# Windowed attention and a squared-ReLU layer on one core: queries and keys of a pair get PSUM tiles of their own, and the first block gets another order

## The chip, the cores and the metric

The kernel runs on one core of one Trainium2 chip. Its time is the device time of one execution in microseconds (us), taken as the median of several runs. A profile of one execution stands beside it; its span runs from the first to the last instruction and is a little shorter than the time of the same execution. In the profile's rows PE is the matrix engine (TensorE), PEld its weight loads, DVE is VectorE, ACT is ScalarE, POOL is GpSimd, SP the engine that issues the DMAs here; SPq is SP's queue.

## The reference

```python
# q, k, v: (8, 8, 576, 64) float32;  w_in: (512, 2048), w_out: (2048, 512) float32
scores = q @ k.transpose(0, 1, 3, 2) / sqrt(64)
rel = pos[:, None] - pos[None, :]
scores = where((rel >= 0) & (rel < 64), scores, -1e9)      # causal, window of 64
attn = softmax(scores)                                     # over the last axis
x = (attn @ v).transpose(0, 2, 1, 3).reshape(4608, 512)    # heads side by side
h = maximum(x @ w_in, 0)
out = (h * h) @ w_out                                      # (4608, 512) float32
```

## The kernel before

**Tiles and blocks.** The 4608 tokens are cut into 36 tiles of 128 tokens. Two tiles make a pair (p = 0 to 17), two pairs a block of 512 tokens (g = 0 to 8). Pairs 8 and 15 are "tails": they hold the last 64 tokens of eight sequences and are loaded with more, smaller DMAs. Everything is computed in fp16 with sums in float32.

**Attention of a tile i.** Keys and queries are loaded, cast to fp16, and turned, so that the head dimension lies on the partitions. `S_` makes the scores: 16 small matmuls of 64x64, with keys as weights and queries as the moving operand. `expo` takes the exponential on ACT, `keep` lays the mask on it on DVE. (For tiles 0 to 3 the mask is instead added by two matmuls ahead of the scores.) `V` multiplies with the values, whose extra column of ones gives the sum; `norm` divides on DVE and writes x. Then x is turned, which gives xT, the moving operand of the first layer.

**How things are turned.** For pairs 0 to 6 (`AHEAD = 7`), `T` turns keys and queries on PE: 16 transposes into one PSUM tile of two banks, 8 for the keys, 8 for the queries. Four copies take them out, one for each tile's keys (`ck`, into kT) and queries (`cq`, into qT). The two tokens that lie side by side in a partition after the load must be put in order again. The key copy does that as it writes (neighbours in PSUM go to every second column). The query copy writes its columns as they come, and the tile is noted in `mixed`; `S_` then reads the queries of such a tile in steps of 64 elements. From pair 7 on, `dma_k` and `dma_q` turn keys and queries by DMA, and `S_` reads the queries in a row. In the same way x is turned on PE (`X`, then `copy_xT`) for tiles 0 to 15, that is for blocks 0 to 3, and by one DMA for each pair (`dma_xT`) from block 4 on.

**Two stages.** The first stage is a list of words, `FIRST`, written out by hand: each word is one step, with an optional engine behind a slash. The order of the words is the order of the instructions in each engine's queue; all DMAs are in SP's. The stage loads and scales `w_in` (`fw`, `w`), runs the attention of blocks 0 to 2, the first layer of blocks 0 and 1 (`U`, with `r` for the ReLU and `s` for the square), and the second layer of block 0 (`O`). `W` is a run of matmuls whose results nobody reads. The second stage is a loop over g = 2 to 9. In each round it lists events with a time between 0 and 1, sorts them and emits them: the second layer of block g-1 (`out_seven`, in 14 steps with its stores), the first layer of block g (16 calls of `UP`, from 0.05 on), the attention of block g+1, and the loads of pairs 2g+4 and 2g+5.

**What takes turns.** Scores, attention sums, turned keys and queries and turned x all draw on one PSUM pool of two tiles of two banks each (`ps_att`). The results of `U`, `O` and `W` draw in turn on two pools of two banks each (`either_pool`). Copies of one PSUM tile by ACT and DVE follow one another in program order.

**SP's order in a round g = 2** (x of block 3 is still turned on PE): turn pair 7 (0.06), load keys, queries and values of pair 8 (0.14), turn pair 8 (0.52), load pair 9 (0.60), store a half of block 1's output (about 0.82), store the other half (about 0.96). In the rounds from 3 on, the DMA that turns x stands at 0.275 and 0.735, behind the loads at 0.14 and 0.60.

The events of attention and of loading, as they stand in the loop:

```python
ev += [(t + 0.02, lambda a=a: sc(a)), (t + 0.021, lambda b=b: sc(b)),
       (t + 0.25, lambda a=a: va(a)), (t + 0.251, lambda b=b: va(b)),
       (t + dx, lambda a=a: to_xT(a)), (t + dx + 0.0001, lambda b=b: to_xT(b))]
...
ev.append((t + 0.06, lambda a=a: (dma_k(a), dma_q(a))))
...
ev.append((t + 0.14, lambda a=a: load(a + 1)))
```

Of the kernel before, what the change touches and what calls it, by code (L numbers as in the profile page):

```python
# [14 lines left out]

SQ_ACT = (0, 2, 4, 6, 8, 10, 12, 14)
FIRST = '''
fv2 fk0 fq0 vc2/D fq1 kc0/A fk1 kc1/A qc1/D fv1 qc0/D h0 T0 W7 qc2 fv0 vd2 fv3 cq0/A ck0/D fw2 ck1
qc3/D fw1 S0 vc1 cq1 kc3/A kc2 S1 W5 ea0 vc0/D fw3 vd0/D eb0 fw0 ea1 vd1/D V0 W5 eb1 n0 V1 T1 n1
h2 vc3/D X0 W9 cq3/A ck2/D ck3 cq2 x0 X1 h4 w2.0/P w2.2 S2 x1/A fq2 vd3 w2.1 S3 ea2 w2.3 eb2 U0.4  # L20
ea3 w1.2/P w1.1 w1.0/A w1.3 V2 U0.5 eb3 n2 V3 r0.5 U0.3 n3 r0.4 w3.2/P s0.4/A w3.0/P X3 X2 w3.3/A
x3 U0.2 x2 r0.3 fk2 s0.5 s0.3/A U1.4 w3.1 r0.2/D U1.6 r1.4 s0.2 U0.6 w0.3/P r1.6 w0.1 fq3 w0.0/A
U1.2 s1.4 s1.6/A r0.6/D qc5 fv4 U0.7 qc4/A s0.6 U1.7 r1.2/D kc5 kc4/A fv5 s1.2 r0.7 w0.2/P T2
r1.7/D fv7 qc6 U1.1 ck4 cq4 ck5/D vc4 S4 r1.1 s0.7 U1.3 fk3 vd4 e4 cq5 h6 U1.0 fk5 s1.7/A vc5 m4
r1.3 S5 vd5 s1.1 e5 V4 fq4 U0.1 h8 n4 qc7 r1.0 U1.5 s1.3/A m5 kc7 fv6 vc7/A r0.1/D V5 kc6 X4 n5
U0.0 fv8 x4/A s1.0/A X5 r0.0/D T3 fk4 x5/A r1.5/D s0.1/A U2.5 fq5 ck7 vc6 s1.5 cq7/A U2.2 qc9
ck6/D r2.5 vd7 s0.0 U2.0 s2.5/A vd6 cq6 fv9 r2.2 S7 r2.0/D S6 fo1 U2.4 e6 s2.2 fo0 s2.0 U2.7 e7
fo2 m6 fo3 U2.3 qc11 r2.4 m7 qc8 r2.7 V6 V7 s2.4/A n6 vc8 U2.1 s2.7/A kc9 n7 kc8/A X6 U2.6 r2.1 x6
r2.3/D kc10/A X7 T4 qc10/A x7 s2.1 s2.3/A o6 U3.0 r2.6/D ck9 fv10 kc11 U3.6 ck8 s2.6 o4 cq8/A
r3.0/D o7 U3.7 vc9/A cq9 s3.0/A vd9 h10 U3.2 r3.6/D r3.7/D U3.1 r3.2 o0 s3.7 s3.6/A T5 o5 r3.1 o2  # L30
U3.4 o1/A ck11/D o3 s3.2/A ck10/D U3.5 o11 fq6 s3.1/A cq10 vd8 U3.3 r3.4/D cq11 s3.4/A S8 o10
r3.5/D S10 e8 fv14 O2.0 s3.5 o12 h12 e10 O2.1 m8 vc10 fv12 O1.0 o8/A o13 m10 fv11 r3.3 vd10 V8
s3.3/A S9 n8 O0.0 o9/A ws0.1 e9 fv13 O1.1 o15/A fk6 O0.1 m9 o14/A O1.2 qc13/A fv15 vc11 vc14/A
vd11 S11 V10 e11 O0.2 n10 vc12/A O1.3 ws0.3 fkq15 ws0.2 kc12 ws1.1 X8 oe1 st1 X10 O2.2 m11 vc13/A
ws1.3 qc12/A O3.0 x8 vd13 ws2.1 kc13/A O3.1 fkq14 vc15 x10 V11 ws1.2 vd14 V9 n11 O0.3 n9 vd15 T6
qc15 ws0.0 O2.3 kc15 cq13/A ck12/D oe0 st0 vd12 O3.2 cq12 ck13 ws2.3 X9 kc14 X11 ws1.0 x9/A O3.3
qc14 oe2 st2 x11 ws2.0 oe3 st3 ws2.2
'''


# [1 line left out]
def kernel(  # L42
# [70 lines left out]
    def tail_seq(i):  # L113

        return 4 * TAILS.index(i // 2) + i % 2 * 2
# [25 lines left out]
    def two_tiles():  # L141
        return stage.tile([P, 2, H, D], FP32, name="kq_st", tag="st2", bufs=6)
# [18 lines left out]
        for n in range(2):  # L161
            sts[nm, 2 * p + n] = st[:, n]

    def fetch_tail(p):

        for nm, src in (("k", k), ("q", q), ("v", v)):
            for i in (2 * p, 2 * p + 1):
                b = tail_seq(i)
                if nm == "q":
                    if i % 2 == 0:  # L170
                        st = two_tiles()
                    sts[nm, i] = st[:, i % 2]
                    for n in range(2):
                        fetch_rows(sts[nm, i], src, b + n, S - 64, 64, 64 * n)
                else:
                    st = two_tiles()
                    sts[nm, i] = st
                    for n in range(2):
                        fetch_rows(st[:, n], src, b + n, S - 128)

# [172 lines left out]
    def att_bank(name, dtype=FP32):  # L355
        return ps_att.tile([P, 2, 512], FP32, name=name, tag="ps_a")

    scs, avs, xps, tps, mixed = {}, {}, {}, {}, set()

    def T(p):  # L360
        ps = att_bank("qkT_ps")[:].rearrange("p s f -> p (s f)").bitcast(FP16).rearrange(
            "p (s two a t) -> p s a two t", s=2, two=2, a=HP)
        for s, src in enumerate((k16s, q16s)):
            for n in range(2):
                for hp in range(HP):
                    nc.tensor.transpose(out=ps[:, s, hp, n, :],  # L366
                                        in_=src[p][:, n, 2 * hp:2 * hp + 2, :],
                                        identity=ident[:])
        tps[p] = ps

    def k_cols(i):
        c0 = 64 + i % 2 * P
        return kT_of(i // 2)[:, :, c0:c0 + P]

    def qT_of(p):
        if p not in qTs:
            qTs[p] = attw.tile([P, 2, HP, P], FP16, name="qT", tag="qT", bufs=3)
        return qTs[p]

    def q_cols(i):  # L380
        return qT_of(i // 2)[:, i % 2]

    def half_of(i, s):
        c0 = i % 2 * 64
        return tps[i // 2][:, s, :, :, c0:c0 + 64]

    def copy_kT(i, eng=nc.scalar):

        copy(eng, k_cols(i).rearrange("p a (t two) -> p a two t", two=2), half_of(i, 0))

    def copy_qT(i, eng=nc.vector):

        copy(eng, q_cols(i).rearrange("p a (two t) -> p a two t", two=2), half_of(i, 1))
        mixed.add(i)

    def flip(out, in_):
        nc.sync.dma_start_transpose(out=out, in_=in_)
# [15 lines left out]
    def S_(i):  # L413
        sc = att_bank("sc")
        scv = sc[:].rearrange("p a (h b t) -> p a h b t", h=HP, b=2)
        for a in range(2 if i < 4 else 0):
            nc.tensor.matmul(sc[:, a, :], ident[:], minus[i > 0], start=True, stop=False,
                             skip_group_check=True)
        for hp in range(HP):
            for blk in range(2):  # L420
                for hh in range(2):
                    r0 = 64 * hh
                    qT = q_cols(i)[r0:r0 + 64, hp, :]
                    if i in mixed:
                        qT = qT.rearrange("d (two b t) -> d b t two", two=2, b=2)[:, blk]
                    else:
                        qT = qT[:, 64 * blk:64 * blk + 64]
                    nc.tensor.matmul(scv[:, hh, hp, blk, :], keys(i, hp, r0, blk), qT,  # L428
                                     start=i >= 4, stop=True, skip_group_check=i < 4)
        scs[i] = sc  # L430
        pms[i] = attw.tile([P, 2, HP * 2 * 64], FP16, name="pm", tag="pm")
# [57 lines left out]
            h2s[g] = h2pool.tile([P, FFC, 512], FP16, name="h2", tag="h2")  # L489
        return h2s[g]  # L490

    hps_of, hr_of, turns = {}, {}, []

    def either_pool():
        turns.append(len(turns) % 2)
        return ((ps_up, "ps_u"), (ps_out, "ps_o"))[turns[-1]]


    def U(p, j):
# [92 lines left out]
    def out_seven(g):  # L592
# [112 lines left out]
        "fkq": fetch_kq,  # L705
        "fw": fetch_w_in, "fo": fetch_w_out, "w": scale_w_in,  "o": cast_w_out,
        "kc": cast_k, "qc": cast_q, "vc": cast_v, "vd": shift_v,
        "T": T, "ck": copy_kT, "cq": copy_qT, "h": halo,
        "S": S_, "e": expo, "ea": lambda i: expo(i, lo), "eb": lambda i: expo(i, hi),
        "m": keep, "ma": lambda i: keep(i, lo), "mb": lambda i: keep(i, hi),  # L710
        "V": V, "n": norm, "X": X, "x": copy_xT, 
# [11 lines left out]
    def attention(g):  # L723
        c = 4 * g
        ev = []
        dx = 0.34 if g == 3 else 0.275

        def sc(i):
            S_(i)
            expo(i)  # L730
            later(2, lambda: keep(i))
            tick()

        def to_xT(i):
            if g == 3:
                X(i)
                copy_xT(i)
                tick()
            else:
                if i % 2:  # L740
                    dma_xT(i // 2)

        def va(i):
            V(i)
            norm(i)
            tick()

        for h in range(2):
            a, b, t = c + 2 * h, c + 2 * h + 1, 0.46 * h + (0.1 if g == 3 else 0.0)
            ev += [(t + 0.02, lambda a=a: sc(a)), (t + 0.021, lambda b=b: sc(b)),  # L750
                   (t + 0.25, lambda a=a: va(a)), (t + 0.251, lambda b=b: va(b)),
                   (t + dx, lambda a=a: to_xT(a)), (t + dx + 0.0001, lambda b=b: to_xT(b))]
        return ev

    def load(p):
        if p in TAILS:
            fetch_tail(p)
        else:
            for nm in "kqv":
                fetch_two(nm, p)  # L760
        for i in (2 * p, 2 * p + 1):
            if p in TAILS:
                k16s["tail", i] = st16.tile([P, 2, H, D], FP16, name="k16", tag="k16")
                nc.gpsimd.tensor_copy(out=k16s["tail", i][:], in_=sts["k", i][:])
            else:
                cast_k(i)
        for i in (2 * p, 2 * p + 1):
            cast_q(i)
        for i in (2 * p, 2 * p + 1):
            if p in TAILS:  # L770
                for n, vv in enumerate((v_ods, v_evs)):
                    nc.gpsimd.tensor_copy(out=vv[i % NV][:, :, 0:D], in_=sts["v", i][:, n])
            else:
                cast_v(i)
                shift_v(i)

    def loads(p):

        ev = []
        for h in range(2):  # L780
# [3 lines left out]
                if a not in TAILS:  # L784
                    ev.append((t + 0.3, lambda a=a: halo_apart(a)))
            if a + 1 < NCK // 2:
                ev.append((t + 0.14, lambda a=a: load(a + 1)))
        return ev

    def even(steps):  # L790
# [46 lines left out]
```

## Time and profile before

| what | us |
|---|---|
| median of 4 runs (300.78 to 303.2) | 302.16 |
| time of the profiled execution | 303.2 |
| its span | 301.5 |
| PE busy | 284.8 |
| DVE busy | 211.8 |
| ACT busy | 186.9 |
| POOL busy | 115.2 |

The granted clock of PE was 0.999 over the span. The DMA engines were at 0.9 or more of their time up to about 60 us, at 0.6 from 60 to 80 us, and at 0.76 to 1.07 from 80 to 240 us.

Reading help: a row of the chain gives start, duration, and the instruction or DMA that the end of the run goes back to at that moment. A row of a timeline gives start, duration from the first to the last of a group, engine, line, operation and tiles. A busy PE row can hold matmuls that run slower than they might; so the rate of matmuls (duration by count) is looked at beside the busy time.

### The profile page before, as it was taken

The numbers are of one execution on the slowest core, as the hardware profiler recorded it, in microseconds if no ns is written. First come the engines' busy times: TensorE is split into PE (matmuls) and PEld (weight loads), VectorE is DVE, ScalarE is ACT, GpSimd is POOL, SyncE is SP. The second block draws the span as 40 slices with busy tenths as digits, with TensorE's granted clock in tenths as the row PEclk, the third lists the DMA queues.
The fourth block names the chain that finished last, engine by engine and source line by source line (L and its number), as shares of the span: only waits on it lengthen the run. The fifth ranks groups of instructions, "written<-read, shape, count | busy, mean of one in ns | idle before, by whom it ended". The sixth has DMA issues, their size and how long they took to land.

```text
span 301.5 us, 7455 instructions
## 1 busy us (share of the span) xinstructions
PE 284.8 (94%) x3026; PEld 196.7 (65%) x3026; DVE 211.8 (70%) x407; ACT 186.9 (62%) x303; POOL 115.2 (38%) x172
## 2 busy tenths in 40 slices
PE   1989999999999999999999999959999999999995
PEld 0658888855566676666666666636666666666684
DVE  4678888866879568685877578765685867646393
ACT  3557798795484757757675767545757675566510
POOL 1359854683615172745266225350565000000000
PEclk9999999999999999999999999999999999999999
DMA  7999999993399999996998899999999211300133
GB/s 222 324 393 301 284 276 364 309 251 80 123 211 217 166 252 197 205 235 186 229 197 196 158 205 163 217 195 225 223 224 257 64 37 35 140 1 0 72 105 107
DMA packets 151843, 57.64 MB, mean 191 GB/s; under 512 B 128256, under 2 KB 143616, under 8 KB 151808
## 3 DMA queue, kind: packets, MB, share of 16 engines
q1 hardware_dynamic: 151808, 57.16, 78.4%
q8 instruction: 24, 0.39, 0.6%
q14 instruction: 11, 0.09, 0.1%
HBM read 38.80 MB, written 9.44 MB: 160 GB/s over the span
## 4 chain that ended last, share of the span: by engine, by line
PE 90%; DMA 3%; ACT 3%; DVE 2%; issue 0%; SPq 0%; DVEq 0%
PE hps L533 32%; PE opsC L621 9%; PE hps L505 9%; PE opsA L621 9%; PE opsD L621 8%; PE opsB L621 5%; PE sc L428 4%; PE ops L581 4%; PE av L451 4%; PE qkT_ps L366 2%; DMA q_st<-in_q_dram 2%; DMA xT<-x_sb 1%; PE xt_ps L471 1%; ACT kT L270 1%; DVE kT L272 1%; ACT pm L434 1%
## 5 line engine op out<-in xcount | busy, mean ns | idle before, releaser
L533 PE MATMUL hps<-xT,w_in_sb 128*128 128x512 f16 x448 | 112.9, 379 | 4.0 <-DMA xT<-x_sb 3.6
L537 ACT ACTIVATE hrelu<-hps 128x512 f32<-128x512 f32 x112 | 66.8, 597 | 71.8 <-PE hps L533 71.8
L621 PEld LDWEIGHTS <-h 128*128 128x128 f16 x624 | 60.5, 98 | 20.9
L533 PEld LDWEIGHTS <-w_in_sb 128*128 128x128 f16 x448 | 42.3, 98 | 36.8 <-issue 4.4
L543 DVE SCALAR_TENSOR_TENSOR h<-hps,hrelu 128x512 f16<-128x512 f32 x56 | 38.6, 690 | 33.7 <-ACT hrelu L537 33.4
L272 POOL COPY v_od<-v_ev 64x512 f16<-64x512 f16 x52 | 35.0, 675 | 12.2 <-ACT v_ev L270 9.3
L434 ACT ACTIVATE pm<-sc 128x1024 f16<-128x1024 f32 (+1 forms) x40 | 35.6, 936 | 3.9 <-PE sc L428 3.7
L540 ACT ACTIVATE h<-hrelu 128x512 f16<-128x512 f32 x56 | 35.2, 629 | 1.5
L621 PE MATMUL opsA<-w_out_sb,h 128*128 128x256 f16 x240 | 31.0, 273 | 0.0
L621 PE MATMUL opsD<-wb_all,h 128*128 128x256 f16 x240 | 30.9, 273 | 0.0
L621 PEld LDWEIGHTS <-hs_all 128*128 128x128 f16 x256 | 25.0, 98 | 8.6
L505 PE MATMUL hps<-xT,w_in_sb 128*128 128x256 f16 x256 | 30.5, 273 | 0.0
L272 POOL CAST k<-kq_st 128x512 f16<-128x512 f32 x18 | 11.3, 628 | 46.3 <-DMA kq_st<-in_k_dram 46.2
L505 PEld LDWEIGHTS <-w_in_sb 128*128 128x128 f16 x256 | 24.1, 98 | 3.3 <-DVE w_in_sb L274 0.2
L460 DVE TENSOR_TENSOR x_sb<-av,rden 128x512 f16<-128x512 f32 x36 | 24.9, 692 | 1.2
L439 DVE TENSOR_TENSOR pm<-pm,mask_inner 128x1024 f16<-128x1024 f16 x25 | 18.0, 721 | 4.9 <-ACT pm L434 4.9
L272 POOL CAST q<-kq_st 128x512 f16<-128x512 f32 x22 | 14.0, 638 | 12.4 <-DMA kq_st<-in_q_dram 11.7
L643 DVE SCALAR_TENSOR_TENSOR osb_all<-opsD,u 128x512 f32<-128x512 f32 x14 | 9.7, 691 | 11.3 <-PE opsD L621 11.3
L621 PE MATMUL opsC<-w_out_sb,h 128*128 128x256 f16 x128 | 16.4, 273 | 0.0
L621 PE MATMUL opsC<-w_out_sb,hs_all 128*128 128x256 f16 x128 | 16.4, 273 | 0.0
L621 PE MATMUL opsB<-wb_all,hs_all 128*128 128x256 f16 x128 | 16.4, 273 | 0.0
L459 DVE RECIPROCAL rden<-av 128x8 f32<-128x8 f32 x36 | 7.3, 202 | 12.5 <-PE av L451 12.3
(101 smaller groups left out, 377.6 us busy)
## 6 DMA issues: line engine op xcount, KB each, us to landing
kq_st<-in_k_dram SPq DMA_DIRECT2D x26, 256.0 KB, 3.6
kq_st<-in_v_dram SPq DMA_DIRECT2D x24, 256.0 KB, 4.7
out_dram<-osb_all SPq DMA_DIRECT2D x12, 512.0 KB, 3.2
kq_st<-in_q_dram SPq DMA_DIRECT2D x18, 256.0 KB, 4.3
v_st<-in_v_dram SPq DMA_DIRECT2D x16, 256.0 KB, 4.8
k_st<-in_k_dram SPq DMA_DIRECT2D x7, 512.0 KB, 5.5
q_st<-in_q_dram SPq DMA_DIRECT2D x7, 512.0 KB, 6.4
out_dram<-osb_all SPq DMA_DIRECT2D x11, 256.0 KB, 2.4
```

Source lines behind the costliest of these rows:

```text
L272: eng.tensor_copy(out=out, in_=in_)
L428: nc.tensor.matmul(scv[:, hh, hp, blk, :], keys(i, hp, r0, blk), qT, start=i >= 4, stop=True, skip_group_check=i < 4)
L434: nc.scalar.activation(out=pms[i][:, part], in_=scs[i][:, part], func=AF.Exp, scale=1.0 / float(D) ** 0.5)
L439: nc.vector.tensor_tensor(out=pms[i][:, part], in0=pms[i][:, part], in1=mask[:].rearrange("p (o a) r -> p o (a r)", o=1) .to_broadcast([P, ...
L451: nc.tensor.matmul(avs[i][64 * blk:64 * blk + 64, h // 4, h % 4, 0:65], pms[i][:, h % 2, h0:h0 + 64], vv[:, h, 0:65], start=True, stop=True)
L460: nc.vector.tensor_tensor(out=xs[i // 2][:, i % 2], in0=avs[i][:, :, :, 0:D], in1=rden[:].to_broadcast([P, 2, 4, D]), op=ALU.mult)
L505: nc.tensor.matmul(hps[:, f, :], w_in_sb[:, c, (2 * j + f) * P:(2 * j + f + 1) * P], xT_of(p // 2)[:, n0:n0 + 2, c, :], start=(c == 0), st ...
L533: nc.tensor.matmul(hps[:], w_in_sb[:, c, f * P:(f + 1) * P], xT_of(g)[:, :, c, :], start=(c == 0), stop=(c == DMC - 1))
L537: nc.scalar.activation(out=hrelu[:], in_=hps[:], func=AF.Relu)
L540: later(2 if f == 0 else 0, lambda: nc.scalar.activation(out=h2_of(g)[:, f, :], in_=hrelu[:], func=AF.Square))
L543: nc.vector.scalar_tensor_tensor(out=h2_of(g)[:, f, :], in0=hps[:], scalar=0.0, in1=hrelu[:], op0=ALU.max, op1=ALU.mult)
L621: nc.tensor.matmul(rows_of(bank, m), a[:, kk, m * P:(m + 1) * P], w[:, kk], start=(first and kk == 0 and (m == 0 or bank in apart)), stop= ...
```

## The change

- `T` is split into `Tk` and `Tq`. Keys keep a tile of the attention pool, of which they use one bank; queries get a bank of the two pools of `U`, `O` and `W`. Both halves are taken out by one copy of 1024 columns for a pair, where there were two of 512.
- The query copy now puts the columns in order as the key copy does, and `S_` reads the queries of every tile in a row; `mixed` is gone.
- `FIRST` is another order, with other engines for some words. `Tk1` stands right behind `Tk0`, the loads of both pairs' keys come before those of the queries, and there are 42 `W` matmuls in place of 26. In both orders the first `U` follows the scores of tiles 2 and 3. `fkq14` and `fkq15` (the loads for pair 7) stand behind the stores of two tiles.
- In the loop, x of block 3 is turned by DMA (`g == 99` is never true): 16 transposes on PE and 4 copies on DVE go, two DMAs come, at 0.375 and 0.835 of round 2.
- `load` is cut in two. Keys and queries are loaded at 0.14 and 0.60, for a tail pair the keys alone; the rest at 0.30 and 0.76. In rounds from 3 on, that is behind the DMA that turns x (0.275, 0.735); in round 2 the rest stands ahead of it.

The core of the diff, with the start of the new order:

```diff
+fv3 fk0 fk1 W9 vc3 fq0 kc0/D kc1/A fq1 h0 vd3/D Tk0 W3 kc3/A kc2 fv1 ck0 Tk1 W8 qc0 qc1/D fv0 h2
+ck1 Tq0 W11 fv2 cq0 qc2/A fw3 qc3/D S0 fw2 vc1/D fw1 S1 W5 ea0 fw0 vc0/D eb0 vd0/D ea1 vc2 vd1/D
+V0 eb1 Tq1 vd2 n0 cq1/A V1 W3 n1 X0 W3 x0 X1 S3 x1/A w3.0 w3.3/A fq2 w3.1 S2 w3.2 ea3 eb3 U0.6 ea2
+V3 eb2 U0.7 n3 w2.1/A w2.3/A w2.0 V2 w2.2 r0.6 X3 n2 U0.5 r0.7 s0.6/A s0.7 X2 U0.4 x2/A x3 w1.0/P
...
+    def T(p, nm):
+        if nm == "k":
+            bank = att_bank("kT_ps")[:, 0, :]
+        else:
+            pool, tag = either_pool()
+            bank = pool.tile([P, 512], FP32, name="qT_ps", tag=tag)[:]
+        ps = bank.bitcast(FP16).rearrange("p (a two t) -> p a two t", a=HP, two=2)
+        for n in range(2):
+            for hp in range(HP):
+                nc.tensor.transpose(out=ps[:, hp, n, :],
+                                    in_={"k": k16s, "q": q16s}[nm][p][:, n, 2 * hp:2 * hp + 2, :],
+                                    identity=ident[:])
+        tps[p, nm] = ps
...
+    def copy_kT(p, eng=nc.scalar):
+        copy(eng, kT_of(p)[:, :, 64:].rearrange("p a (t two) -> p a two t", two=2), tps[p, "k"])
+    def copy_qT(p, eng=nc.vector):
+        copy(eng, qT_of(p)[:].rearrange("p a (t two) -> p a two t", two=2), tps[p, "q"])
...
-                    if i in mixed:
-                        qT = qT.rearrange("d (two b t) -> d b t two", two=2, b=2)[:, blk]
-                    else:
-                        qT = qT[:, 64 * blk:64 * blk + 64]
+                    qT = qT[:, 64 * blk:64 * blk + 64]
...
-        dx = 0.34 if g == 3 else 0.275
+        dx = 0.34 if g == 99 else 0.275
...
-            if g == 3:
+            if g == 99:
                 X(i)
                 copy_xT(i)
...
-                ev.append((t + 0.14, lambda a=a: load(a + 1)))
+                kq = "k" if a + 1 in TAILS else "kq"
+                ev.append((t + 0.14, lambda a=a, x=kq: load(a + 1, x)))
+                ev.append((t + 0.3, lambda a=a, x=kq: load(a + 1, "kqv"[len(x):])))
```

## The prediction, made before the result was known

> **What bounds the kernel now.** First the busy table of the page, then PE's waits, then the chain, then SP's queue.
>
> ```profile
> PE 284.8 (94%) x3026; PEld 196.7 (65%) x3026; DVE 211.8 (70%) x407; ACT 186.9 (62%) x303; POOL 115.2 (38%) x172
> ```
>
> ```profile
> PE qkT_ps L366 <- ACT k L270: 6.2, 1, 6.2
> PE hps L533 <- DMA xT<-x_sb: 3.6, 1, 3.6
> PE xt_ps L471 <- DVE qT L272: 1.4, 1, 1.4
> PE xt_ps L471 <- ACT kT L270: 0.6, 1, 0.6
> ```
>
> PE is the bound: it idles 16.7 us in all, 6.2 before its first transpose, 3.6 in one wait for x of block 6, 1.4 and 0.6 behind the copies of turned keys and queries. So PE work saved, or one of these waits, counts; work of others counts only where PE waits for it. A busy PE may also run slowly, so the chain comes next (start, duration, what):
>
> ```profile
> 16.07 0.61 ACT qT L270
> 16.68 0.02 issue
> 16.70 0.74 DVE kT L272
> 17.45 0.02 issue
> 17.47 0.75 ACT kT L270
> 18.22 0.02 issue
> 18.24 0.44 DVE qT L272
> 18.68 0.05 issue
> 18.72 0.40 PE xt_ps L471 x4
> ...
> 44.87 1.10 PE sc L428 x32
> ...
> 111.72 0.57 PE sc L428 x32
> ```
>
> The four copies of one PSUM tile run one after the other, 2.6 us, and the next transpose waits for the last. And the same 32 score matmuls take 1.10 us where queries are read in steps of 64 elements (44.87, pairs 0 to 6), 0.57 where they lie in a row (111.72, turned by DMA). Last, SP's timeline where PE waits 3.6 us:
>
> ```profile
> 187.13 3.88 SPq L122 DMA_DIRECT2D kq_st<-in_k_dram  x4
> 191.06 2.90 SPq L122 DMA_DIRECT2D kq_st<-in_q_dram  x4
> 194.00 4.91 SPq L122 DMA_DIRECT2D kq_st<-in_v_dram  x4
> 199.00 1.97 SPq L480 DMA_TRANSPOSE xT<-x_sb  x1
> ```
>
> The second half of block 6's x was ready on DVE at 192.2 us, yet its DMA is issued at 199.00, behind the tail pair's queries and values, and lands at 203.4. PE was free for it at 199.9.
>
> **The change part by part.**
>
> *a. The start up to the first U's: -2.2 (0 to -3.0).* Bytes ahead of `w_in`'s first quarter are the same, so it lands at 17.3 as before. The first transposes of keys still wait for k0 (landed 5.5), about 6.2 to 7.2. k1 comes second (7.05), so `Tk1` runs about 7.9 to 8.8; q0 comes third and lands at about 8.6, where q1 landed before. `W8` and `Tq0` end about 11.1. The one-piece query copy on DVE is not in the trace: two of its like (0.73 for 512 columns out of order) give 1.46, one of 512 in order 0.41 is the floor; I take 1.4, nearest the two, as it writes out of order. `W11` fills that time; scores of tile 0 at 12.5. From there PE does S0, S1, W5, V0, Tq1, V1, W3, X0, W3, X1, S3, S2, by rows (0.55 for the mask pair and 0.29 for scores, 0.65, 0.38, 0.45, 0.38, 0.35, 0.25) 6.0 us, with 0.3 of waits for norm and the xT copy: first U at 18.8, against 21.3. Then the second quarter of `w_in` (20.1) and its scaling hold the third U to 21.9, and the first U of pair 1 starts at 24.3; before, it started at 26.45. So 2.2. The 16 added `W` matmuls (0.11 each, 1.8 us) lie in these waits; uncovered, they would cost that.
>
> *b. Scores of tiles 4 to 11: -2.1 (0 to -2.1).* (1.10 - 0.57)/2 = 0.265 for a tile, by eight. Tiles 0 to 3 are in a, 12 and 13 in e. It is nothing where PE would then wait for ACT or DVE.
>
> *c. The 0.6 wait at 79.1 us: -0.6 (0 to -0.6).* `Tq6` no longer holds the attention bank that the last X waited for.
>
> *d. New waits in the first block: +1.2 (0 to +4).* For five pairs, copies were 2 x 0.74 for keys and 0.41 or 0.60 twice for queries, 2.3 to 2.7 us; now two copies. On ACT, one of 1024 columns is bounded by 0.94 (the exponential of that size) and 2 x 0.74; so the pair costs 2.3 to 2.9, the same. But the words move one relu and square each way: two more of each on ACT (2.5 us), two fewer on DVE, and queries now take a bank from the U's.
>
> ```profile
> 24.00:60.00 36.00, 35.52 (x460) 30.75 (x455) 31.77 (x61) 30.31 (x53) 25.02 (x38) 1.00 1.03 306
> ```
>
> In this row (window, length, then busy PE, PEld, DVE, ACT, POOL) DVE is 88% and ACT 84% busy, DMA full; PE in less time leaves them about 90%. I take a quarter us for each of the five pairs.
>
> [...]
>
> *e. Block 3's x by DMA, at the border of rounds 2 and 3: +1.6 (-1.4 to +3.5).* Off PE go four X (0.45 a pair, 0.9) and the slow half of scores 12 and 13 (0.5). DVE loses 4 x 0.41, off the path. But SP is full in round 2: from 82.12 (keys of pair 7) to 107.7 (values of pair 9) it hardly waits. The new DMA at 0.375 adds 1.7 us of issue (1.23 to 2.88 in the ten rows), all else of the round waits for it. The second stands behind the values of pair 9 and a store: issue at about 107.7 + 1.7 + 0.4 = 109.8. These DMAs land 2.7 to 6.6 us after issue, 4.9 in the middle behind loads: 114.7. PE wants it at 113.1 - 0.9 - 0.5 = 111.7. So PE waits 3.0 and the border is 1.6 later than before. With 2.7 and a quicker queue the wait is nothing (-1.4), with 6.6 it is 4.9 (+3.5).
>
> [...]
>
> *f. Loads behind x in rounds 3 to 7: -3.6 (-1.0 to -3.6).* In round 5 x is issued right behind the tail's keys, at 192.3, when it is ready, and lands 2.7 to 6.6 later, 195 to 198.9, before 199.9. The wait goes. Elsewhere x was waited for by SP itself (134.49, 163.37) or landed in time.
>
> *g. What is late next: +0.4 (0 to +2).* The tail's queries and values and two stores follow x, so SP comes to turn pair 15 at about 204.7 where it was 203.5, and its queries at about 209, landing (2.9, up to 5) by 212 to 214. PE, 3.6 earlier, wants them for tile 30 at 215.7 - 3.6 = 212.1. The next x (pair 15) has the 3.3 us of pair 17's values out of its way, landing at about 228 where PE wants it at 229.
>
> Sum: -2.2 - 2.1 - 0.6 + 1.2 + 1.6 - 3.6 + 0.4 = -5.3. The profiled execution took 303.2 (span 301.5 and 1.7 around it): 297.9. It was the slowest of the four runs; from their median of 302.16 the same step gives 296.9, and I say 297.0.
>
> **The rivals.**
>
> *Everything in time (0.15).* No new wait in the first block, block 3's x lands early, pair 15 too: -2.2 - 2.1 - 0.6 - 1.4 - 3.6 = -9.9, 292.3. For it: SP had gaps of 1 to 2 us in rounds 3 and 4. Against: DMA at 0.92 to 1.37 from 85 to 115 us.
>
> *The DMA engines are the bound from 80 to 230 us (0.13).* Then taking one late transfer away makes the next late: f gives 1.0, e costs 3.5, g 2.0: -2.2 - 2.1 - 0.6 + 1.2 + 3.5 - 1.0 + 2.0 = +0.8, 303.0. For it: the DMA share of 0.97 over 80 to 200 us. Against: PE waits once in this stretch.
>
> *Scores don't get faster (0.05).* If the step is not what made them slow, b, half of a and 0.5 of e go: about -2, 300.
>
> *ACT and DVE become the bound of the first block (0.15), slower.* Ten one-piece copies (five pairs) of up to 1.46 us on in-order queues that are 84 to 88% busy each hold a relu or a square behind them, and with it a PSUM bank that the U after next needs. At 1.0 us of PE for each it is +10 in place of 1.2: -5.3 + 8.8 = +3.5, 305.7. It decides from about 0.9 for each. For it: the row of 24 to 60 us. Against: that row's PE idles 0.5 us only, and a bank is wanted back after four U's, 3.5 us.
>
> **How the numbers follow.** The forecast has 0.52, its own spread 295 to 299. 1% is what a measurement here tells from no change: faster than 299.1 is the forecast and the first rival, 0.67; within 1% are the DMA rival and the scores rival, 0.18; slower 0.15. The range runs from 293.0, short of the first rival's end, to 303.2, past the DMA rival; it leaves out the slower rival and some of the first.
>
> **What would show it.** Right: score rows of 0.57 for 32 from the first tile on; the first U at 18 to 20 us; `opsA` of round 2 by 77 to 78 us; no wait of PE for xT near 196, but one of about 3 us near 111. Wrong: many waits of U's matmuls for relu, square or the copies between 24 and 75 us; PE waiting for qT of pair 15; a second late x behind round 5. The weakest terms are d and e: d, since a chain of short waits is not seen in advance, and e, since it hangs on one landing.

## The result, and the profile after

The changed kernel takes 303.19 us (median of 43 runs, 300.98 to 306.74), the kernel before 301.82 (64 runs, 299.84 to 306.42). The ratio is 1.0044, with a 95% interval of 1.0029 to 1.006: half a per cent slower, which is within the 1% that the prediction took for no change. Forecast was 297.0, 1.7% faster. The profiled execution of the changed kernel took 305.2 us with a span of 303.3, so it is, like that of before, one of the longer ones.

Where the gain went is told best by the rounds. The table gives the first half step of the second layer (`opsA` in PE's timeline) in each round of the loop, worked out as differences of its starts; the first column is the time at which round 2 starts, that is, the length of the first block.

| profiled execution | first block | round 2 | round 3 | 4 | 5 | 6 | 7 | 8 |
|---|---|---|---|---|---|---|---|---|
| before | 80.75 | 31.48 | 28.88 | 28.88 | 28.88 | 32.67 | 28.21 | 26.04 |
| after | 77.27 | 31.08 | **37.45** | 28.88 | 28.88 | 29.48 | 28.74 | 26.04 |

The first block is 3.5 us shorter, round 6 is 3.2 shorter, and round 3 is 8.6 longer. PE's waits in the changed kernel (waiting instruction, releaser, us in total, times, longest):

```profile
PE hps L526 <- DMA xT<-x_sb: 6.0, 2, 5.6
PE warm L545 <- DVE mask_first L249: 2.7, 1, 2.7
PE hps L526 <- DVE h L536: 1.6, 3, 0.8
```

The old waits of 6.2 (first transposes), 1.4 and 0.6 (copies) are gone, shorter or filled with `W` matmuls. The wait for x is back, longer. Its place in the chain of the changed kernel:

```profile
107.41 0.57 SPq L651
...
108.02 6.97 DMA xT<-x_sb
...
115.04 1.89 PE hps L526 x4
116.93 1.71 PE opsA L614 x8
118.63 1.71 PE hps L526 x4
120.34 1.10 PE opsA L614 x8
```

The DMA that turns the second half of block 3's x is issued at 108.02 and lands 6.97 us later. What follows runs at half its rate: four matmuls of 512 columns and eight of 256 take 1.71 us where the rows of other rounds have 0.86 and 0.87. The windows of the same stretch (length, busy PE, PEld, DVE, ACT, POOL, then the granted clock, DMA share, GB/s) show why:

```profile
110.00:112.00 2.00, 0.00 (x0) 0.00 (x0) 1.97 (x4) 0.31 (x1) 1.90 (x3) 1.00 2.46 192
112.00:114.00 2.00, 0.00 (x0) 0.00 (x0) 2.00 (x3) 0.00 (x0) 1.87 (x3) 0.96 0.11 29
114.00:116.00 2.00, 0.96 (x3) 0.41 (x4) 1.01 (x2) 0.00 (x0) 1.46 (x2) 0.50 1.13 364
116.00:118.00 2.00, 2.00 (x10) 1.08 (x8) 0.00 (x0) 0.60 (x1) 0.00 (x0) 0.50 1.08 239
118.00:120.00 2.00, 2.00 (x7) 0.91 (x6) 0.00 (x0) 1.11 (x2) 0.00 (x0) 0.50 1.07 242
```

The granted clock falls to 0.50 at about 113.8, while PE idles, and stays there for 6.8 us (worked out from windows of 1 us, which show 0.92, six times 0.50 and 0.66 from 113 to 121). Round 3 is 37.45 - 28.88 = 8.57 too long: 5.64 of wait, and the other 2.9, which fits the matmuls at half rate up to 120.7. SP's timeline before that DMA:

```profile
104.68 2.47 SPq L121 DMA_DIRECT2D kq_st<-in_v_dram  x2
107.26 0.72 SPq L651 DMA_DIRECT2D out_dram<-osb_all  x1
108.02 2.58 SPq L477 DMA_TRANSPOSE xT<-x_sb  x1
```

x itself was ready on DVE at 104.1; values of pair 9 and a store stood ahead of its DMA. Why it then took 6.97 us to land is not shown. In round 6 the wait for x is gone, as forecast. In SP's timeline there, x now goes ahead of the tail's queries (and of its values, which follow at 201.90):

```profile
189.30 4.60 SPq L121 DMA_DIRECT2D kq_st<-in_k_dram  x4
196.94 1.24 SPq L477 DMA_TRANSPOSE xT<-x_sb  x1
198.22 3.63 SPq L121 DMA_DIRECT2D kq_st<-in_q_dram  x4
```

### The profile page after: what moved, and what is told of

Its sections match the earlier page's. It is cut to its first block, busy times and chain, and to the rows that moved or that the text cites. A ratio compares the mean times of both kernels' runs of the same rounds, so it can differ in the third digit from the quotient of the medians.

```text
span 303.3 us, 7447 instructions
## 1 busy us (share of the span) xinstructions
PE 286.6 (95%) x3026; PEld 196.5 (65%) x3026; DVE 216.3 (71%) x392; ACT 190.0 (63%) x300; POOL 117.9 (39%) x172
## 4 chain that ended last, share of the span: by engine, by line
PE 73%; DVE 13%; ACT 7%; DMA 5%; issue 1%; SPq 0%
PE hps L526 30%; PE opsC L614 9%; PE opsD L614 7%; PE opsA L614 6%; PE hps L498 5%; PE opsB L614 5%; DMA xT<-x_sb 4%; PE av L448 3%; DVE hs_all L602 2%; PE sc L425 2%; DVE pm L436 2%; ACT pm L431 2%; DMA k_st<-in_k_dram 1%; DVE x_sb L457 1%; ACT h L517 1%
## 5 line engine op out<-in xcount | busy, mean ns | idle before, releaser
L526 PE MATMUL hps<-xT,w_in_sb 128*128 128x512 f16 x448 | 114.6, 384 | 7.6 <-DMA xT<-x_sb 6.0
L269 POOL COPY v_od<-v_ev 64x512 f16<-64x512 f16 x51 | 39.2, 768 | 7.3 <-ACT v_ev L267 4.1
L614 PE MATMUL opsA<-w_out_sb,h 128*128 128x256 f16 x240 | 32.1, 279 | 0.0
L457 DVE TENSOR_TENSOR x_sb<-av,rden 128x512 f16<-128x512 f32 x36 | 24.9, 692 | 1.2
L436 DVE TENSOR_TENSOR pm<-pm,mask_inner 128x1024 f16<-128x1024 f16 x25 | 20.2, 807 | 6.4 <-ACT pm L431 6.3
L269 POOL CAST q<-kq_st 128x512 f16<-128x512 f32 x22 | 15.7, 714 | 17.8 <-DMA kq_st<-in_q_dram 17.7
L269 POOL CAST v_ev<-kq_st 128x512 f16<-128x512 f32 x16 | 11.3, 704 | 23.7 <-DMA kq_st<-in_v_dram 22.0
```

Source lines behind the costliest of these rows:

```text
L269: eng.tensor_copy(out=out, in_=in_)
L436: nc.vector.tensor_tensor(out=pms[i][:, part], in0=pms[i][:, part], in1=mask[:].rearrange("p (o a) r -> p o (a r)", o=1) .to_broadcast([P, ...
L457: nc.vector.tensor_tensor(out=xs[i // 2][:, i % 2], in0=avs[i][:, :, :, 0:D], in1=rden[:].to_broadcast([P, 2, 4, D]), op=ALU.mult)
L526: nc.tensor.matmul(hps[:], w_in_sb[:, c, f * P:(f + 1) * P], xT_of(g)[:, :, c, :], start=(c == 0), stop=(c == DMC - 1))
L614: nc.tensor.matmul(rows_of(bank, m), a[:, kk, m * P:(m + 1) * P], w[:, kk], start=(first and kk == 0 and (m == 0 or bank in apart)), stop= ...
```

## The experiments

Theory 1, after this reading: the first block and the split loads gain, and block 3's late x with the half clock behind it eats the gain. Theory 2: the DMA engines are the bound from 80 to 230 us, and a wait taken away comes back elsewhere. Theory 3: x of block 3 is late only because the new first block brings PE there earlier.

**Block 3's x back on PE.**

```diff
-        dx = 0.34 if g == 99 else 0.275
+        dx = 0.34 if g == 3 else 0.275
...
-            if g == 99:
+            if g == 3:
                 X(i)
                 copy_xT(i)
```

> The changed kernel with block 3's x turned on PE again (16 transposes and 4 copies back, two DMAs gone); all else as changed. Theory 1 (the loss is the late second half of block 3's x: 5.6 us of wait, then about 2.5 us of matmuls at half clock): both go and 0.9 us of transposes come back, 303.2 - 8.1 + 0.9 = 296.0 (295 to 297.5), no wait for xT near 109 us, granted clock 0.99 or more throughout. Theory 2 (the DMA engines are the bound from 80 to 230 us and the wait only moves to a later x): 300 or more, with a wait of 3 us or more for xT in a later round.

Measured: 296.74 (296.38 to 298.73), ratio to before 0.983 (0.978 to 0.988). Rounds: 76.02, then 31.98, 28.91, 28.88, 28.88, 29.70, 28.46. Its longest waits:

```profile
PE warm L545 <- DVE mask_first L249: 2.7, 1, 2.7
PE hps L526 <- DVE h L536: 2.0, 4, 0.9
PE kT_ps L373 <- DVE k L269: 1.4, 1, 1.4
```

No row names xT, and no wait has moved to a later round. The one edit is worth 6.5 us, and theory 2 falls: the DMA engines are busy (0.92 of their time from 80 to 200 us in the changed kernel), but they are not what the rounds wait for once this transfer is out of the way.

**Block 3's x by DMA in the kernel before, alone.** The same two lines, the other way, in the old kernel.

> The kernel before with one edit: block 3's x turned by DMA. Theory 1: the second half of that x lands after PE wants it here too, though SP starts the round 1.7 us earlier against PE than in the changed kernel: wait of 2 to 5 us near 113 us, less 0.9 of transposes, and if the clock falls 2 to 3 us more: 303 to 307. Theory 3 (x is late only because the new first block brings PE there earlier): no wait, 301.0.

Measured: 305.68 (303.82 to 307.38), ratio 1.013 (1.007 to 1.019). Round 3 is 32.91. PE's timeline of this kernel (start, duration, engine, line, tiles, wait):

```profile
114.97 1.88 PE L533 MATMUL hps<-xT,w_in_sb 128*128 128x512 f16 x4 [2.18 <-DMA xT<-x_sb]
...
118.35 1.07 PE L533 MATMUL hps<-xT,w_in_sb 128*128 128x512 f16 x4
```

The wait comes with the old first block too, 2.18 us long, and half clock behind it (0.50 from 115.0 to 118.4). Theory 3 falls: the new order makes the wait longer, but does not alone bring it. The profiled execution is the shortest of the four; one of the others, 304.92 us, has a granted clock of 1.000, so a loss can come without the half clock too.

**The new first block alone.** Here x of block 3 is on PE, and the loads are in one piece.

```diff
-                kq = "k" if a + 1 in TAILS else "kq"
-                ev.append((t + 0.14, lambda a=a, x=kq: load(a + 1, x)))
-                ev.append((t + 0.3, lambda a=a, x=kq: load(a + 1, "kqv"[len(x):])))
+                ev.append((t + 0.14, lambda a=a: load(a + 1, "kqv")))
```

> The new first block alone (turned keys and queries in tiles apart, queries read in a row, the new order); in the loop x of block 3 on PE and the loads in one piece, as before. Theory 1: first round starts 3.5 us earlier, scores of tiles 12 and 13 give 0.5, the wait for x of block 6 stays at 3 to 4 us: 297.8 (297 to 299). Theory 2 (DMA is the bound): what the first block gains comes back as a longer wait for x of block 6, 5 us or more: 300 to 302.

Measured: 297.99 (296.93 to 300.38), ratio 0.987 (0.980 to 0.993). Round 2 starts at 76.61. The wait for x of block 6 is 1.1 us, not 3 to 4, and round 6 is 30.19.

**The split loads alone, in the kernel before.** The new `load` and `fetch_tail`, called at 0.14 and 0.30 as in the change.

> The kernel before with one edit: the loads cut in two, values (and a tail's queries) behind x. Theory 1: the wait of 3.6 us for x of block 6 goes, 0.7 us comes elsewhere: 298.9 (298 to 299.7). Theory 2 (DMA is the bound): the wait comes back at the next x: 301 to 302.

Measured: 301.72 (300.78 to 303.39), ratio 1.000 (0.997 to 1.003). A miss for the 298.9 that I expected. No wait for xT is left in its profile, round 6 is 29.13, yet the time is that of before. Either 3.6 us was not what before usually waits, or something is lost elsewhere.

**The kernel before, profiled once more.**

> The kernel before, unchanged, profiled once more. With the loads in one piece, two other kernels waited 1.0 and 1.1 us for x of block 6, where the profiled execution of before waited 3.6. Theory 4 (that execution was a long one, the usual wait is about 1 us, and so the split of the loads had little to gain): wait of 0.5 to 2 us, time 300.5 to 302. Theory 1 as predicted (the wait is a steady 3.6): 3 to 4 us.

Measured: 302.16 in one execution, first block 81.67, round 6 30.43. Two of its waits:

```profile
PE xt_ps L471 <- DVE qT L272: 1.4, 1, 1.4
PE hps L533 <- DMA xT<-x_sb: 1.4, 1, 1.4
```

With the loads in one piece, five profiled executions of four programs waited 3.6, 1.4, 1.1, 1.0 and, further down, 0.6 us for this x. The one that I had read was the longest. And round 7 is 28.21 in all of these, 28.46 to 28.87 in all ten kernels with the loads split, which are 0.25 to 0.66 longer there. Together the two leave little for the split to gain.

The same profile shows something else. Its first block is 0.9 longer than in the profile that I had read, although it has the same wait of 1.42 us for the turned queries. What differs is the clock, which falls to 0.50 for 3.4 us from about 20.5 on:

```profile
18.59 0.40 PE L471 MATMUL xt_ps<-ident,x_sb 128*128 128x128 f16 x4 [1.42 <-DVE qT L272]
...
21.18 1.89 PE L505 MATMUL hps<-xT,w_in_sb 128*128 128x256 f16 x8
```

```profile
20.00:22.00 2.00, 2.00 (x26) 1.20 (x23) 1.43 (x3) 1.73 (x4) 1.15 (x1) 0.63 1.05 387
22.00:24.00 2.00, 2.00 (x24) 1.29 (x23) 0.28 (x2) 0.96 (x2) 1.43 (x1) 0.52 1.08 366
```

In the profile that I had read, the clock is 1.00 there, and the row reads:

```profile
21.31 1.05 PE L505 MATMUL hps<-xT,w_in_sb 128*128 128x256 f16 x8
```

**The wait filled with matmuls, 56 and 30 of them.** They stand ahead of block 3's first matmul and write a tile that nobody reads.

```diff
+    def warm_att(n):
...
+        if g == 3:
+            ev += [(0.055, lambda: warm_att(56))]      # 30 in the second kernel
```

> The changed kernel with 56 idle matmuls of 256 columns (6.1 us at full clock) on PE between the first half step of block 2's second layer and the first matmul of block 3, in the attention pool; results read by nobody. Theory 1 (of the 8.5 us that the round of block 3 is too long, 5.6 are the wait and about 2.5 to 3 are matmuls at half clock that the long idle brings on): the wait is filled, the granted clock stays at 1.00 between 108 and 122 us, and the time falls by 2 to 3, less up to 0.5 that the filling outlasts the wait: 300.7 (300 to 301.5). Rival (the slow matmuls after the wait have another cause): 303 to 304.

> The changed kernel with 30 idle matmuls (3.3 us) in the wait, where 56 (6.1 us) outlasted it and gained nothing. If the half clock costs 2 us or more by itself, the clock stays at 1.00 and the time is 300.8 (300 to 301.8). If the clock is worth little, 302.5 to 303.5.

Measured: with 56, 303.34 (302.41 to 303.63), ratio 1.005 (1.002 to 1.007), no gain; with 30, 300.45 (299.12 to 302.43), ratio 0.998 (0.995 to 1.000). In the first, x had landed at 107.1 + 6.1 = 113.2, and the filling went on to 115.5, so that it cost 2.3 us of its own. The second, in PE's timeline and by its windows:

```profile
108.81 3.44 PE L552 MATMUL warm<-mask_first,ident 128*128 128x256 f16 x30
113.64 1.02 PE L526 MATMUL hps<-xT,w_in_sb 128*128 128x512 f16 x4 [1.39 <-DMA xT<-x_sb]
```

```profile
112.00:114.00 2.00, 0.61 (x5) 0.27 (x3) 1.97 (x3) 0.00 (x0) 1.87 (x3) 1.00 0.97 300
114.00:116.00 2.00, 2.00 (x15) 1.27 (x13) 0.43 (x1) 0.97 (x2) 1.51 (x2) 1.00 1.21 237
```

x is as late as ever (5.9 us from the start of the round to the first matmul of block 3, against 6.7 in the changed kernel's profile), but the clock stays at 1.00 (0.994 in one of the ten executions), and 2.7 us by the medians, 2.0 by the ratios to before, are gained by matmuls that compute nothing. Up to 0.8 of it may be the earlier landing; the rest, 1.2 to 2.7 us, is the half clock's price, apart from the wait's. The 56 kept the clock too (0.999 or 1.000 in all ten), but what they outlasted the data by cost as much.

**Values of pair 9 behind x.**

```diff
-                ev.append((t + 0.3, lambda a=a, x=kq: load(a + 1, "kqv"[len(x):])))
+                ev.append((t + (0.42 if a == 8 else 0.3),
+                           lambda a=a, x=kq: load(a + 1, "kqv"[len(x):])))
```

> The changed kernel with one event moved: the values of pair 9 are loaded at 0.88 of round 2, behind the DMA that turns the second half of block 3's x, where they stood at 0.76 ahead of it. Theory 1 (that DMA is late because of what stands ahead of it in SP's queue): issue near 105.4 in place of 108.0, wait 2 to 3 in place of 5.6, no or a shorter stretch of half clock: 297.8 (296.5 to 299.5). Rival (the DMA engines are so full that it lands no earlier): 302.5 to 303.5.

Measured: 298.40 (297.13 to 302.8), ratio 0.987 (0.983 to 0.990). PE's row at the border:

```profile
111.27 1.02 PE L526 MATMUL hps<-xT,w_in_sb 128*128 128x512 f16 x4 [1.26 <-DMA xT<-x_sb]
```

The DMA is issued at 106.72 and lands 4.42 later, round 3 is 30.32, and the clock stays in the profiled execution. In two of the ten executions, 301.74 and 302.80 us, the granted clock is 0.989 as in the changed kernel; they were not profiled, so how long PE waited there is not known. One event moved by 0.12 of a round gives 4.8 us by the medians: the place in the queue was the main cause.

**Pair 7 loaded ahead of the first store.**

```diff
-... O2.3 oe0 st0 ... qc13 fkq14 qc12 ... O1.2 fkq15 n11 ...
+... O2.3 fkq14 fkq15 oe0 st0 ... qc13 qc12 ... O1.2 n11 ...
```

> The changed kernel with two words moved in the first block: the loads of keys and queries of pair 7 (two tiles) stand ahead of the first store of an output tile, where they stood behind two stores. Theory 1 (the turning of pair 7 starts SP's round 2, 3.1 us after PE's in the changed kernel and 1.4 before, and all of the round hangs on it): SP starts 1 to 2 us earlier against PE, the wait of 5.6 us for block 3's x shrinks by as much, the half clock may stay: 301.3 (300 to 302.5). Rival (DMA engines or POOL set the pace): 303.

Measured: four executions, 300.92, 300.92 and 301.67 at a granted clock of 0.989 to 0.994, and 296.03 at 0.999; no interval can be given. SP now starts round 2 at 78.22, 1.4 us after PE's 76.86, as it does in the kernel before; in the changed kernel it is 3.1 after. In the profiled execution the wait is 3.8 us and half clock follows. The fourth execution is as fast as the kernels in which x comes in time; it was not profiled, so whether x did so there stays open. Three of the four lie about the expected 301.3; how often the fast one comes, four executions do not decide.

**Only the second half of block 3's x on PE.**

```diff
-            if g == 99:
+            if i in (14, 15):
...
-                   (t + dx, lambda a=a: to_xT(a)), (t + dx + 0.0001, lambda b=b: to_xT(b))]
+                   (t + (0.34 if a == 14 else dx), lambda a=a: to_xT(a)),
+                   (t + (0.34 if a == 14 else dx) + 0.0001, lambda b=b: to_xT(b))]
```

> The changed kernel with the second half of block 3's x (tiles 14 and 15) on PE, the first half still by DMA. Theory 1 (only the second half is late): no wait at the border, PE has 0.45 us less to do than with both halves on PE: 296.3 (295.5 to 297.5). Rival (the first half's DMA pushes all later transfers of the round, and the turning of tail pair 8 comes late): 298 or more.

Measured: 297.30 (297.07 to 297.57), ratio 0.984 (0.980 to 0.988). Round 3 is 29.26 with no wait for xT. The first half by DMA does no harm, and no good that shows: against both halves on PE (296.74) the ratios to before are 0.984 and 0.983.

**Both moves together: pair 7 earlier, pair 9's values behind x.**

> The changed kernel with both moves: pair 7 loaded ahead of the first output store, and pair 9's values behind the DMA that turns the second half of block 3's x. Theory 1: no wait at the border of rounds 2 and 3 (0 to 0.7), and PE spared all 16 transposes: 296.3 (295.5 to 297.5). Rival (the DMA engines are too full, a wait of 1 us or more stays): 298 or more.

Measured: 296.53 (296.11 to 297.08), ratio 0.984 (0.982 to 0.987). SP issues x at 104.51, 1.1 us after it is ready on DVE (103.4), behind one store; round 2 is 30.31, round 3 29.09. All of block 3's x goes by DMA, and PE waits 0.3 us for it. So the edit can be made to cost nothing; against x on PE (296.74) it gains nothing that these runs can tell.

**Queries read in a row, alone, in the kernel before.**

```diff
-        copy(eng, q_cols(i).rearrange("p a (two t) -> p a two t", two=2), half_of(i, 1))
-        mixed.add(i)
+        copy(eng, q_cols(i).rearrange("p a (t two) -> p a two t", two=2), half_of(i, 1))
```

> The kernel before with the query copy putting its columns in order and scores reading queries in a row; still one PSUM tile and four copies a pair, old order. Theory 1 (the slow scores are the step of 64 elements): 32 score matmuls take 0.57 us in place of 1.10 in the first block; 14 tiles at 0.265 are 3.7, less about 1 for nine DVE copies that take 0.73 in place of 0.41: 299 (298 to 300). Rival (PE then waits for ACT or DVE as long): 301 to 302.

Measured: 301.63 (299.96 to 302.71), ratio 1.0015 (0.9985 to 1.0045). The rival holds. The scores do run faster (16 in 0.34 us in place of 0.60), and PE waits for the copies instead:

```profile
PE xt_ps L470 <- DVE qT L272: 1.9, 1, 1.9
PE sc L427 <- DVE qT L272: 1.6, 3, 0.7
PE xt_ps L470 <- ACT kT L270: 1.0, 1, 1.0
PE sc L416 <- DVE qT L272: 1.0, 1, 1.0
```

These are 5.5 us; before, the same four kinds were 2.4 (1.4, 0.4, 0.6 and none). 3.1 of the 3.7 that the faster scores should save goes there. Part of the loss in this profile is the clock, which is at 0.50 for 3.4 us behind the wait of 1.9; but the five executions at 0.999 or 1.000 have a median of 301.11, against 300.93 for those of the kernel before beside them, so nothing is gained at full clock either. All four copies of a pair are still in one line behind one PSUM tile, and each query copy is longer (0.74 on DVE and 0.75 on ACT in the chain at 16 to 19 us, where before had 0.44 and 0.61).

**Queries read in steps again, in the new order** (the changed kernel with block 3's x on PE, and this).

```diff
-        copy(eng, qT_of(p)[:].rearrange("p a (t two) -> p a two t", two=2), tps[p, "q"])
+        copy(eng, qT_of(p)[:].rearrange("p a (two t) -> p a two t", two=2), tps[p, "q"])
...
-                    qT = q_cols(i)[r0:r0 + 64, hp, :]
-                    qT = qT[:, 64 * blk:64 * blk + 64]
+                    if i // 2 < AHEAD:
+                        qT = qT_of(i // 2)[r0:r0 + 64, hp, :].rearrange(
+                            "d (two n b t) -> d n b t two", two=2, n=2, b=2)[:, i % 2, blk]
+                    else:
+                        qT = q_cols(i)[r0:r0 + 64, hp, 64 * blk:64 * blk + 64]
...
```

> The changed kernel with block 3's x on PE (296.7), and queries copied as they come and read in steps again, in the new order with its tiles apart. Theory 1 (PE is the bound of the new first block, so reading in a row is worth its PE time there): 32 score matmuls take 1.10 us again, 14 tiles at 0.265 are 3.7, less shorter copies: 299.5 (298.3 to 300.5). Rival (as in the old order, where reading in a row alone gained nothing, PE waits for ACT and DVE instead): 296 to 297.5.

Measured: 300.08 (299.03 to 301.83), ratio 0.993 (0.990 to 0.997), against 0.983 with queries in a row: 3.3 us by the medians, 3.1 by the ratios. (The step is 128 elements here, since a pair's queries lie in one tile; it was 64.) The chain has the scores at their old price, and the copies are shorter (0.69 on DVE, 1.02 on ACT, in place of 1.31 and 1.32):

```profile
43.10 1.10 PE sc L428 x32
```

So reading in a row is worth some 3 us in the new order and nothing in the old one: here it pays only where the copies no longer hold PE.

## Why the prediction was wrong, point by point

**The failed step is e**, the border of rounds 2 and 3. It named the right place, the right transfer and the right cause (SP's queue), and put the whole at +1.6. Rounds 2 and 3 together went from 60.36 to 68.53, +8.2 in the profiles: 5.6 of wait and 2.9 of half clock, less 0.4 in round 2, where the sum had 3.0 of wait less 1.4 of work. By the medians, taking the edit back (303.19 to 296.74) is worth 6.5. Four parts of it were off:

- SP's start. I let SP begin round 2 1.4 us after PE, as before. The new order puts the loads of pair 7 behind two stores, and it begins 3.1 after: 80.38 against 77.27. That is 1.7, and with the loads ahead of the stores SP does start 1.4 after PE.
- The landing. I took 4.9; it was 6.97, longer than any of the ten DMAs of that kind in the trace of before (6.6). That is 2.1, and its cause stays open. The wait was thus 5.6 and not 3.0; PE's own need came 1.2 later than reckoned (32.1 after the start of round 2, not 31.0).
- The half clock, 2.9. It is not in the sum at all: each wait is priced at its length. The one profile that I had read has a wait of 3.6 us with the clock at 1.00 behind it, which gave no reason to price more. The short filling gains 2.0 to 2.7, most of it by keeping the clock.
- The saving on PE, -1.4 (four X and two faster scores). Round 2 is only 0.4 shorter: PE now waits 0.76 for DVE early in it, where DVE's last four changes of `w_out` take 2.71 us, 1.42 before. What holds back the rest of the 1.0 is not shown.

The range of the whole, 293.0 to 303.2, reaches just to the result, but a clear gain was forecast and a small loss came; e's own range ended at +3.5 (by its own numbers 109.8 + 6.6 - 111.7 is a wait of 4.7, not 4.9, and the end +3.3), far below what was measured.

**a to d** hold as a sum, in part by luck: -3.7 said, -3.5 in the profile, but a gave 0.7 less and the rest 0.5 more than said. In the eight other kernels with the new first block and queries in a row round 2 starts at 76.0 to 77.6. a alone was too good. The first U starts at 19.86, not 18.8, and the first U of pair 1 at 24.9, not 24.3: a gain of 1.5, not 2.2. Of the 1.1 at the first U, 0.4 is a slip in the sum: the rows listed add up to 6.4 us, not 6.0. The rest goes with DVE's queue, which the prediction had not followed: in the chain, DVE is busy from the query copy at 11.46 through casts and four copies of values (0.58, 0.62, 0.29, 0.29) up to 16.05, and only then does the norm of tile 0 start. PE idles only 0.3 there, as said, because `W` matmuls stand in the wait. b was nearly right in size (3.1 to 3.3 us for all 14 tiles, with the parts in a and e and less the shorter copies, against 3.7), and its condition "nothing where PE would then wait for ACT or DVE" is what the old order shows. c went, with a wait of 0.8 for the key copy in its place. d was small as said: PE idles 0.8 us from 24 to 60 us in the changed kernel, with ACT at 33.0 of 36 us:

```profile
24.00:60.00 36.00, 35.23 (x501) 29.77 (x499) 31.90 (x55) 33.04 (x53) 26.86 (x40) 1.00 1.00 297
```

The one-piece copies took 1.31 on DVE and 1.32 on ACT; 1.4 and the span from 0.94 to 1.48 had been said. The same 1024 columns, written as they come in the kernel with queries read in steps again, took 0.69 and 1.02.

**f** was mis-sized. The mechanism is right: with x ahead of the tail's loads no wait of 1 us or more for this x is left. But 3.6 came from one execution; the four other profiles have 0.6 to 1.4. Alone the split gains 0.0 (-0.9 to +0.9 by its interval), since round 7 gives 0.25 to 0.5 back. On top of the new first block it is 297.99 against 296.74, whose intervals overlap.

**g** was right: a wait of 0.4 for x at the start of round 7, and none for pair 15.

**The rivals.** The DMA rival gave 303.0, very near the result, and that is luck: with the one late transfer out of the way no other came late, its term for e was 3.5 where 6.5 was lost, and its loss of 2.0 in round 7 was 0.5. A right number is no proof of a mechanism. The slower rival (copies on busy engines) did not happen. The price of the transposes (eight in a row take 0.45 us on PE in the chain of the changed kernel, and 16 by DMA 1.23 to 2.88 us of issue in the ten rows of before) did not decide: where x goes by DMA in time, the two ways take the same time (296.5 and 296.7).

## What to carry to other kernels

Price a DMA that an engine waits for by its place in its queue, where here one event moved, with no transfer's size changed, was worth 4.8 us: list all that stands ahead of it, when that queue starts, and the longest landing seen (here the one that counted was longer still), and set it ahead of whatever nobody waits for yet. A wait of PE can cost more than its length through the clock: here a stretch of 3.4 us at half clock, some 1.7 us if PE has work all through it, followed waits of 1.42 to 3.79 us in five profiles, and a stretch twice as long came with the wait of 5.64. Price both, and where the wait can't go, try idle matmuls that end before the data lands: here 30 of them left the granted clock at 0.998 or more in nine of ten executions. A stall that is read from one execution is one draw: look for it in a second profile before it enters the sum at full size.

## What the runs showed of the hardware that was not expected

The clock does not follow from the length of PE's idle time alone. Six profiles have a stretch of half clock while PE still has work. At the border of rounds 2 and 3 it came with waits of 2.18, 3.79 and 5.64 us; in the first block it came behind the wait for the turned queries, 1.42 us long in two profiles (the kernel before profiled again, and the split loads alone) and 1.86 us in one (queries in a row in the kernel before). None came behind the same wait of 1.42 us in the first profile of before, nor behind 3.63 us in that profile, nor behind 1.26 and 1.39 us. What else decides whether a stretch follows, the runs do not show.

The stretches have the same length in five of the six profiles. Worked out from windows of 1 us (0.76, 0.50, 0.50 and 0.54 from 20 to 24 us in the second profile of before, for one), they last 3.4 us there and 6.8, twice that, in the changed kernel. From these an estimate of how many an execution had can be made by its mean granted clock: 3.4 us at half clock are 0.6% of 300 us, so 0.994 is taken for one, 0.989 for two. By that estimate each of the 44 executions of the changed kernel whose clock is on record has one (25, median 302.57) or two (19, median 304.36). Of the kernel before, 15 of 64 have one. With the new first block and block 3's x on PE or in time (the kernels of 296.74, 297.30, 296.53 and 300.08), none of 22 executions is below 0.998.

In the first 10 us the granted clock and the rate of the matmuls do not agree: the windows say 1.00, but eight `W` matmuls take 1.71 us at 8.86 in the chain of the changed kernel, 0.21 each, where the 30 of the short filling take 3.44, 0.11 each.
